# A build-time planner that counts all DMA queues as one pipe, lets row pairs interrupt dense products, and runs an FFN unit of the last chunk later

## The chip, the cores and the metric

The kernel runs on one core of a Trainium2 chip. The metric is the device time of one execution in microseconds (us), as the median of several runs. A profiled execution gives the trace: its span runs from the first to the last instruction, and its own time is a little longer than the span.

## The reference

A transformer layer for 2048 tokens of width 640: attention in a sliding window of 256 tokens with 32 heads of 20, then a feed-forward network (FFN) of width 1536 with a gated GELU, both behind a layer norm and with a residual. Everything is float32.

```python
def _A_ref(x, wqkv, wo):                       # H = 32; Dh = 20; W = 256
    qkv = (x @ wqkv).reshape(B, S, 3, H, Dh).transpose(2, 0, 3, 1, 4)
    q, k, v = qkv[0], qkv[1], qkv[2]
    scores = einsum("bhqd,bhkd->bhqk", q, k) * (Dh ** -0.5)
    mask = (idx[:, None] - idx[None, :] >= 0) & (idx[:, None] - idx[None, :] < W)
    p = softmax(where(mask, scores, -1e9), axis=-1)
    o = einsum("bhqk,bhkd->bhqd", p, v)
    return o.transpose(0, 2, 1, 3).reshape(B, S, D) @ wo
def _B_ref(x, w_gate, w_up, w_down):
    return (gelu(x @ w_gate) * (x @ w_up)) @ w_down

h  = x + _A_ref(layernorm(x), A_wqkv, A_wo)
h2 = h + _B_ref(layernorm(h), B_w_gate, B_w_up, B_w_down)
```

## The kernel before

**Dense products.** Every float32 operand of a large product is split into two float16 parts, high and low, and the product is three float16 matmuls (high by high, high by low, low by high) summed in PSUM (the helper `products`). These are the dense products: `qk` for the queries and keys of a chunk of 256 tokens, `vproj` and `wo_block` for a block of 128 tokens, and the FFN's. There are 16 blocks and 8 chunks. In rows of the trace the float16 weights are `w0`, `w1`, `w2`, `w3` (q, k, v, o) with `h` or `l` behind, and `xh`, `xl`, `oh`, `ol` are the parts of the normed input and of the attention's output.

**Attention.** A block has 8 units of 4 heads. For each unit the scores are computed twice: once to find each row's maximum (`maxima`, rows `ps<-kT,qT`), and once, with that maximum subtracted by two extra rows of qT, transposed for the exponential (`scores`, rows `ps<-qT,kT`). Two units use the two halves of TensorE's 128 rows at the same time; two such units are a row pair, mostly one of maxima for a later block and one of scores, 24 matmuls in all. Each of the two writes its own set of three PSUM banks, and a pair starts only when both sets are free. Behind maxima VectorE (DVE) masks and reduces (`mxs`) and so frees the set; behind scores ScalarE (ACT) takes the exponential into `pt` and frees the set, GpSimd (POOL) masks `pt`, and the values follow: 48 matmuls `ps<-pt,v` for two units, on columns of TensorE in groups of 32 (`value_lane`).

When the 8 units of a block have their maxima, `max_rows` splits them into `m16`, TensorE transposes them (`ps<-ident,m`), ACT copies the result to `mT`, and two DMAs on ACT's queue write it into the extra rows of qT. Only then can the block's first scores run.

**Turning.** `turned` transposes a block of x, of the attention's output (o) or of the normed h for use as a matmul operand: ACT casts to the high part `sph`, POOL subtracts to get the low part `spl`, and two transposing DMAs on SP's queue write both. There is one `sph` and one `spl`, so a cast waits until the transposing DMA of the cast before has read.

**FFN.** It works on 4 chunks of 512 tokens (c) and 3 groups of 512 inner columns (fg), 12 units (c, fg), each with `gate_up` and `down`. Except for two of them, gate and up use seven block products instead of eight on sums of weights and of tokens (`gate_up_sums`). The sums of a chunk's tokens are `token_sums`, written to `tTh`, `tTl` or to a part of the room of `kT`, which is free then. The list `SEQ` sets the order of the units; `feed_forward` issues the gate/up of one unit and then the down of the unit before. The weights of group 0 are split a second time late in the list, when `("up", 3, 2)` is done, since their room was used for group 2. The first FFN units also serve as filling for TensorE at the end of the attention.

**What sets the order of the work.** Nothing is ordered by hand. The program is written by lanes, Python generators whose steps each issue a few instructions, and while it is built a planner, the class `Clock`, keeps a planned time for each engine: `Engine.cost` gives each instruction's duration, `issue` advances the engine's time beyond the operands' planned times, and a DMA is planned to land some time after its issue. A lane's step is taken when its operands are ready in this plan. The order in which lanes are asked at each step is `order = early + outs + trans + sides + turn`; `turn` holds the three lanes that feed TensorE: `rows` (row pairs), `values` and `dense`. Once the v weights are split it was:

```python
elif pos["open"]:
    turn = [dense, values, rows]
elif nc.mode == "row":
    turn = [values, dense, rows]
elif nc.mode == "col":
    turn = [dense, rows, values]
else:
    turn = [rows, values, dense]
if W["v"].ready and not pos["open"] and pos["since"] and row_need() < nc.t["tensor"] + SOON:
    turn = [rows, values]
```

`pos["open"]` is 1 while a dense product is unfinished, `pos["since"]` counts products since the last row pair, and `row_need()` is the planned time at which the next pair could start. With `SOON = 2.0`, dense work is held back at a product's end when a pair is due within 2 us. The result is a fixed order of instructions on each engine; nothing is scheduled on the chip. All instructions are recorded through one helper, so their line in the trace is L211 (L226 in the changed file).

Of the kernel before, what the change touches and what calls it, by code (L numbers as in the profile page):

```python
# [55 lines left out]
class Clock:  # L56
# [6 lines left out]
    def __init__(self, nc):  # L63
        self.nc = nc
        self.t = dict.fromkeys(self.NOW, 0.0)
        self.wr, self.rd, self.rings = {}, {}, {}
        self.warm, self.win, self.use = False, 0, 0.0
        self.mode, self.half = "full", 0
        self.moved = dict.fromkeys(self.NOW, 0.0)
        self.port = {"vector": deque(maxlen=6), "gpsimd": deque(maxlen=6)}  # L70
        for e in self.NOW:
            setattr(self, e, Engine(self, e))
# [98 lines left out]
    def shares(reads, writes):  # L171
        big = [a for a in reads if a.free_size() > 1 and a.space != PSUM]
        return len(big) > 1 or (len(big) == 1 and not any(a.space == PSUM for a in reads)
                                and writes[0].free_size() > 8 and writes[0].space != PSUM)

    def issue(self, eng, cost, reads, writes, move=False):
        start = self.t[eng]
        boxes = [self.box(a) for a in reads], [self.box(a) for a in writes]
        for a, (k, b) in zip(reads, boxes[0]):
            start = max(start, self.latest(self.wr, k, b, eng))  # L180
            if a.space == PSUM:
                start = max(start, self.others(a, eng))
        for k, b in boxes[1]:
            start = max(start, self.latest(self.wr, k, b, eng), self.latest(self.rd, k, b, eng))
        if not move and (eng == "gpsimd" or eng == "vector" and self.shares(reads, writes)):
            for a, z in self.port["vector" if eng == "gpsimd" else "gpsimd"]:
                if a <= start < z:
                    start = z
            self.port[eng].append((start, start + cost))
        if move:  # L190
            self.t[eng] = start + move
            self.moved[eng] = max(self.moved[eng], start + 0.2) + cost
            end = self.moved[eng] + 1.7
        else:
            end = self.t[eng] = start + cost
        for k, b in boxes[0]:
            self.note(self.rd, k, b, eng, end)
        for k, b in boxes[1]:
            self.note(self.wr, k, b, eng, end)


class Engine:
# [23 lines left out]
    def cost(self, op, out, ins):  # L226
        n = out.free_size()
        if op.startswith("dma_start"):
            size = n * out.partition_size() * mybir.dt.size(out.dtype)
            return size / (300e3 if mybir.dt.size(out.dtype) == 4 else 150e3)  # L230
        half = mybir.dt.size(out.dtype) == 2 and ins and mybir.dt.size(ins[0].dtype) == 2
        if self.name == "tensor":
            n = ins[1].free_size()
# [31 lines left out]
def block_kernel(ctx: ExitStack, tc: tile.TileContext, x, wqkv, wo, wg, wu, wd, out):  # L265
    nc = Clock(tc.nc)
# [75 lines left out]
    FFBACK = dict(split_lane=0.4, scale_lane=0.4, chunk_lane=0.3)  # L342
    EARLY = 0.6
    PACE = 1.0
    SOON = 2.0

    def need(*reads, slots=(), when=None, eng="tensor"):

# [217 lines left out]
    W = {}  # L566
# [80 lines left out]
    def products(n, term, ready=None, at_=None):  # L647


        ps = [at_[0]] if at_ else []  # L650
        col = at_[1] if at_ else 0

        def start(i):
            if ready and not ready(i):
                return INF
            t = nc.ready([x for ab in term(i) for x in ab], "tensor")
            return t if ps else max(t, room("mm"))

        for i in range(n):
            yield ("tensor",), lambda i=i: start(i)  # L660
            if not ps:
                ps.append(bank("mm"))
            pos["open"] = 1
            m = term(i)
            for k, (l, r) in enumerate(m):
                if k:
                    yield pe()
                o = ps[0][:, col:col + r.free_size()]
                nc.tensor.matmul(o, l, r, start=(i == 0 and k == 0),
                                 stop=(i == n - 1 and k == len(m) - 1))  # L670
                pos["dense"] += r.free_size()
        pos["open"] = 0
        pos["since"] += 1
        return o

    ffk = const.tile([P, FG, 5], F32, name="ffk")
# [330 lines left out]
    def row_lane():  # L1007
        while True:
            yield ("tensor",), row_need
            gens = []  # L1010
            pos["since"] = 0
            for s, (f, x) in enumerate(row):
                (maxq if f is maxima else scoreq).remove(x)
                gens.append(f(*x, row_set(s)))
# [157 lines left out]
    def wo_out(j, nh, ps):  # L1172
# [6 lines left out]
        if b.halves < 2:  # L1179
# [6 lines left out]
    NCH = S // (CB * P)  # L1186
    hts, ga, tT = {}, {}, {}
    flags = set()
    SEQ = [(0, 0), (1, 0), (0, 1), (1, 1), (1, 2), (0, 2), (2, 2), (3, 2), (3, 1), (2, 1), (2, 0),
           (3, 0)]  # L1190
    POOL = (0, 1, 1, 0)

# [69 lines left out]
    def gate_up_sums(c, fg):  # L1262
# [9 lines left out]
        for w in ws:  # L1272
            tiles = {}
            for n, terms in enumerate(STEPS):
# [9 lines left out]
                for h in range(2):  # L1284
                    for m, x in enumerate(names):
                        yield ("tensor",), lambda: start(*x)
                        new = ps is None
                        if new:
                            ps = bank("mm")
                        pos["open"] = 1  # L1290
                        l, r, k = x
                        for p, (lw, rt) in enumerate(parts(w.part(l, k), tokens(c, r, k))):
                            if p:
# [5 lines left out]
                            pos["dense"] += 256  # L1299
                tasks.append(combine(n, w is ws[1], c, fg, ps, tiles, gels))  # L1300
                yield
        pos["open"] = 0

    def combine(n, up, c, fg, ps, tiles, gels):

# [408 lines left out]
    while dense.alive or sides or side or outs or tasks:  # L1714
# [11 lines left out]
        if not W["v"].ready:  # L1726
            att_first = maxq or nc.t["vector"] < nc.t["tensor"]
            turn = [rows, values, dense] if att_first else [dense, rows, values]
        elif pos["open"]:
            turn = [dense, values, rows]  # L1730
        elif nc.mode == "row":
            turn = [values, dense, rows]
        elif nc.mode == "col":
            turn = [dense, rows, values]
        else:
            turn = [rows, values, dense]
        if W["v"].ready and not pos["open"] and pos["since"] and row_need() < nc.t["tensor"] + SOON:
            turn = [rows, values]
        order = early + outs + trans + sides + turn
        for lane in order:  # L1740
            if lane.alive and lane.start(now):
# [59 lines left out]
```

## Time and profile before

| | before |
|---|---|
| median of 3 runs | 1013.43 us (1011.65 to 1015.23) |
| the profiled execution | 1011.27 us, span 1009.6 us |
| mean granted clock of TensorE | 0.988 |
| PE (matmuls) busy | 953.7 us, 94% |
| DVE, ACT, POOL busy | 730.7, 484.1, 238.1 us |
| DMA | 106.89 MB; SP's queue (q1) 35.8%, ACT's queue (q10) 4.4% of 16 engines |

Attention, with the projections between, runs to some 615 us of the span; the rest is FFN. Idle time is given with what ended it. A busy PE is not always a fast one: the granted clock says whether it ran at full or at half speed.

### The profile page before, as it was taken

How to read it: one execution, taken by the hardware profiler on the slowest of the kernel's cores; microseconds unless marked ns; L12 is line 12 of the kernel's file. 1: busy time of each engine (PE TensorE's matmuls, PEld its weight loads, DVE VectorE, ACT ScalarE, POOL GpSimd, SP SyncE). 2: the span in 40 equal slices, each digit the busy share in tenths (PEclk: the TensorE clock that was granted, in tenths of full speed). 3: DMA queues.
4: the chain of work that ended last, by engine and by line, in shares of the span. 5: the costliest groups of instructions: out<-in, count | busy, mean ns of one | idle time of the engine just before them, and what ended most of it. 6: DMA issues, size and time to landing. Idle time of an engine off the chain costs nothing.

```text
span 1009.6 us, 27335 instructions
## 1 busy us (share of the span) xinstructions
PE 953.7 (94%) x11687; PEld 737.4 (73%) x11687; DVE 730.7 (72%) x1393; ACT 484.1 (48%) x711; POOL 238.1 (24%) x336
## 2 busy tenths in 40 slices
PE   3997998899899999999998999999999999999998
PEld 2885666677687777777555656888788778888886
DVE  6986698686675666665998745979977969663563
ACT  6634656555556555655677663654322224231120
POOL 5201233544543433333434320000111200000000
PEclk9998998999999999999999999999999999999999
DMA  9446685543662533527467014252334323000002
GB/s 338 121 121 187 162 219 125 114 111 69 121 145 55 129 86 78 105 59 202 122 158 170 16 27 157 69 181 87 98 80 132 92 66 83 31 15 1 1 1 105
DMA packets 109305, 106.89 MB, mean 106 GB/s; under 512 B 59136, under 2 KB 79872, under 8 KB 107264
## 3 DMA queue, kind: packets, MB, share of 16 engines
q1 hardware_dynamic: 86080, 94.40, 35.8%
q10 hardware_dynamic: 23104, 10.75, 4.4%
q8 instruction: 91, 1.49, 0.6%
q14 instruction: 30, 0.25, 0.1%
HBM read 71.11 MB, written 20.97 MB: 91 GB/s over the span
## 4 chain that ended last, share of the span: by engine, by line
PE 54%; DVE 22%; DMA 10%; ACT 6%; issue 5%; POOL 2%; SPq 1%; ACTq 1%; DVEq 0%; POOLq 0%
PE ps L211 54%; DVE gel L211 4%; DVE mxs L211 3%; DVE kT L211 3%; DVE ps L211 2%; DMA lxn<-h_dram 2%; ACT pt L211 2%; DVE ht L211 2%; DMA qT<-mT 1%; DMA h0l<-spl 1%; ACT wsl L211 1%; DVE wu L211 1%; DMA wsl<-in_wd_dram 1%; DMA wsl<-in_wg_dram 1%; DVE gu L211 1%
## 5 line engine op out<-in xcount | busy, mean ns | idle before, releaser
L211 ACT ACTIVATE pt<-ps,esc 128x1536 f32<-128x1536 f32 (+2 forms) x128 | 186.4, 1460 | 77.3 <-PE ps L211 64.2
L211 POOL TENSOR_SCALAR_AFFINE_SELECT pt<-pt 128x512 f32<-128x512 f32 x240 | 149.2, 644 | 288.5 <-ACT pt L211 283.5
L211 DVE TENSOR_REDUCE mxs<-ps 128x4 f32<-128x1024 f32 (+1 forms) x128 | 150.5, 1179 | 2.0
L211 PEld LDWEIGHTS <-kT 62*128 62x128 f16 (+1 forms) x1920 | 126.6, 96 | 33.9 <-issue 11.6
L211 DVE COPY_PREDICATED ps<-mask,ps 128x512 f32<-128x512 int32 x112 | 77.4, 692 | 81.7 <-PE ps L211 80.8
L211 DVE TENSOR_TENSOR gel<-gel,ps 128x512 f32<-128x512 f32 x140 | 93.3, 684 | 46.9 <-PE ps L211 43.4
L211 PE MATMUL ps<-qT,kT 62*128 62x128 f16 x1440 | 102.6, 219 | 14.4 <-DMA qT<-mT 8.0
L211 PEld LDWEIGHTS <-gu 128*128 128x128 f16 x888 | 87.2, 99 | 38.2 <-issue 4.0
L211 PEld LDWEIGHTS <-wu 128*128 128x128 f16 x1080 | 105.6, 98 | 12.5 <-DVE wu L211 0.3
L211 PE MATMUL ps<-kT,qT 60*128 60x128 f16 x1440 | 106.2, 219 | 8.7 <-DVE mxs L211 6.5
L211 PEld LDWEIGHTS <-qT 60*128 60x128 f16 x1440 | 82.0, 95 | 41.6 <-issue 41.2
L211 PE MATMUL ps<-pt,v 128*21 128x128 f32 x2880 | 92.3, 276 | 2.4 <-ACT mT L211 1.5
L211 PEld LDWEIGHTS ps<-pt,v 128*21 128x21 f32 x2880 | 74.2, 101 | 16.8 <-issue 7.4
L211 DVE SCALAR_TENSOR_TENSOR ht<-ps,ffk,ht 128x320 f32<-128x320 f32 x96 | 51.8, 548 | 37.0 <-PE ps L211 35.3
L211 PE MATMUL ps<-xh,w0h 128*128 128x256 f16 x200 | 56.5, 282 | 5.9 <-ACT w0h L211 5.4
L211 PE MATMUL ps<-xh,w1h 128*128 128x256 f16 x200 | 56.4, 283 | 0.3 <-DVE qks L211 0.3
L211 PE MATMUL ps<-xl,w0h 128*128 128x256 f16 x200 | 56.4, 282 | 0.0
L211 PE MATMUL ps<-xl,w1h 128*128 128x256 f16 x200 | 56.1, 282 | 0.0
L211 PEld LDWEIGHTS <-ah 128*128 128x128 f16 x448 | 43.5, 98 | 16.8 <-issue 0.2
L211 PE MATMUL ps<-xh,w1l 128*128 128x256 f16 x200 | 55.7, 281 | 0.0
L211 PE MATMUL ps<-xh,w0l 128*128 128x256 f16 x200 | 55.6, 282 | 0.0
L211 ACT ACTIVATE gel<-gel,ffk 128x512 f32<-128x512 f32 x40 | 28.6, 719 | 45.8 <-DVE gel L211 45.7
(243 smaller groups left out, 2256.2 us busy)
## 6 DMA issues: line engine op xcount, KB each, us to landing
wsl<-in_wd_dram SPq DMA_DIRECT2D x28, 320.0 KB
wsl<-in_wg_dram SPq DMA_DIRECT2D x33, 256.0 KB
qk<-qks ACTq DMA_DIRECT2D x64, 128.0 KB
wsl<-in_wu_dram SPq DMA_DIRECT2D x30, 256.0 KB
qT<-qk SPq DMA_DIRECT2D x16, 320.0 KB
kT<-qk SPq DMA_DIRECT2D x16, 320.0 KB
ht<-in_x_dram SPq DMA_DIRECT2D x16, 320.0 KB
h_dram<-ht SPq DMA_DIRECT2D x16, 320.0 KB
```

Source lines behind the costliest of these rows:

```text
L211: r = real(*args, **kw)
```

## The change

Three things change in the planner and one list in the kernel.

- Every DMA, of whichever queue, takes its transfer time from one shared list of used stretches (`pipe`), starts 0.4 us after its issue, and lands 1.3 us after its transfer, or 3.3 us for a small one. The rates become 330 and 300 KB/us, and 90 for a transposing DMA, in place of 300 and 150 for each queue by itself.
- `turn` is always `[rows, values, dense]` once v is split. `pos["open"]`, `pos["since"]` and `SOON` are gone: a row pair or values may start between any two matmuls of a dense product, and dense work is never held back.
- In `SEQ` the unit (2, 1) moves from the tenth to the seventh place; (2, 2), (3, 2) and (3, 1) come one place later.

```diff
--- before.py
+++ after.py
@@ -66,7 +66,7 @@
         self.wr, self.rd, self.rings = {}, {}, {}
         self.warm, self.win, self.use = False, 0, 0.0
         self.mode, self.half = "full", 0
-        self.moved = dict.fromkeys(self.NOW, 0.0)
+        self.moved, self.used = dict.fromkeys(self.NOW, 0.0), []
         self.port = {"vector": deque(maxlen=6), "gpsimd": deque(maxlen=6)}
         for e in self.NOW:
             setattr(self, e, Engine(self, e))
@@ -173,6 +173,21 @@
         return len(big) > 1 or (len(big) == 1 and not any(a.space == PSUM for a in reads)
                                 and writes[0].free_size() > 8 and writes[0].space != PSUM)
 
+    def pipe(self, at, cost):
+
+        gaps = []
+        for a, z in self.used:
+            if at < a:
+                gaps.append((at, min(a, at + cost)))
+                cost -= gaps[-1][1] - at
+                if cost <= 0:
+                    break
+            at = max(at, z)
+        if cost > 0:
+            gaps.append((at, at + cost))
+        self.used = sorted(self.used[-150:] + gaps)
+        return gaps[-1][1]
+
     def issue(self, eng, cost, reads, writes, move=False):
         start = self.t[eng]
         boxes = [self.box(a) for a in reads], [self.box(a) for a in writes]
@@ -189,8 +204,8 @@
             self.port[eng].append((start, start + cost))
         if move:
             self.t[eng] = start + move
-            self.moved[eng] = max(self.moved[eng], start + 0.2) + cost
-            end = self.moved[eng] + 1.7
+            self.moved[eng] = self.pipe(max(self.moved[eng], start + 0.4), cost)
+            end = self.moved[eng] + (1.3 if cost > 0.05 else 3.3)
         else:
             end = self.t[eng] = start + cost
         for k, b in boxes[0]:
@@ -227,7 +242,9 @@
         n = out.free_size()
         if op.startswith("dma_start"):
             size = n * out.partition_size() * mybir.dt.size(out.dtype)
-            return size / (300e3 if mybir.dt.size(out.dtype) == 4 else 150e3)
+            if op.endswith("transpose"):
+                return size / 90e3
+            return size / (330e3 if mybir.dt.size(out.dtype) == 4 else 300e3)
         half = mybir.dt.size(out.dtype) == 2 and ins and mybir.dt.size(ins[0].dtype) == 2
         if self.name == "tensor":
             n = ins[1].free_size()
@@ -342,7 +359,6 @@
     FFBACK = dict(split_lane=0.4, scale_lane=0.4, chunk_lane=0.3)
     EARLY = 0.6
     PACE = 1.0
-    SOON = 2.0
 
     def need(*reads, slots=(), when=None, eng="tensor"):
 
@@ -660,7 +676,6 @@
             yield ("tensor",), lambda i=i: start(i)
             if not ps:
                 ps.append(bank("mm"))
-            pos["open"] = 1
             m = term(i)
             for k, (l, r) in enumerate(m):
                 if k:
@@ -669,8 +684,6 @@
                 nc.tensor.matmul(o, l, r, start=(i == 0 and k == 0),
                                  stop=(i == n - 1 and k == len(m) - 1))
                 pos["dense"] += r.free_size()
-        pos["open"] = 0
-        pos["since"] += 1
         return o
 
     ffk = const.tile([P, FG, 5], F32, name="ffk")
@@ -1008,7 +1021,6 @@
         while True:
             yield ("tensor",), row_need
             gens = []
-            pos["since"] = 0
             for s, (f, x) in enumerate(row):
                 (maxq if f is maxima else scoreq).remove(x)
                 gens.append(f(*x, row_set(s)))
@@ -1186,7 +1198,7 @@
     NCH = S // (CB * P)
     hts, ga, tT = {}, {}, {}
     flags = set()
-    SEQ = [(0, 0), (1, 0), (0, 1), (1, 1), (1, 2), (0, 2), (2, 2), (3, 2), (3, 1), (2, 1), (2, 0),
+    SEQ = [(0, 0), (1, 0), (0, 1), (1, 1), (1, 2), (0, 2), (2, 1), (2, 2), (3, 2), (3, 1), (2, 0),
            (3, 0)]
     POOL = (0, 1, 1, 0)
 
@@ -1287,7 +1299,6 @@
                         new = ps is None
                         if new:
                             ps = bank("mm")
-                        pos["open"] = 1
                         l, r, k = x
                         for p, (lw, rt) in enumerate(parts(w.part(l, k), tokens(c, r, k))):
                             if p:
@@ -1299,7 +1310,6 @@
                             pos["dense"] += 256
                 tasks.append(combine(n, w is ws[1], c, fg, ps, tiles, gels))
                 yield
-        pos["open"] = 0
 
     def combine(n, up, c, fg, ps, tiles, gels):
 
@@ -1726,16 +1736,8 @@
         if not W["v"].ready:
             att_first = maxq or nc.t["vector"] < nc.t["tensor"]
             turn = [rows, values, dense] if att_first else [dense, rows, values]
-        elif pos["open"]:
-            turn = [dense, values, rows]
-        elif nc.mode == "row":
-            turn = [values, dense, rows]
-        elif nc.mode == "col":
-            turn = [dense, rows, values]
         else:
             turn = [rows, values, dense]
-        if W["v"].ready and not pos["open"] and pos["since"] and row_need() < nc.t["tensor"] + SOON:
-            turn = [rows, values]
         order = early + outs + trans + sides + turn
         for lane in order:
             if lane.alive and lane.start(now):
```

The instructions are the same, but ACT loads its tables of functions 4 times instead of 8; their order changes on every engine. Three places follow, before and after apart.

First, PE at block 2. The row with `ident16` transposes the block's maxima; the rows of `w1h` and `w1l` are the dense product of keys in which it stands, and `LDWEIGHTS qT` with what follows begins the pair that has the block's first scores. Before:

```order
L211 MATMUL ps8_73<-ident16_77,m16_2073 64x128
L211 LDWEIGHTS w1h_281
L211 MATMUL ps8_73<-xl_674,w1h_281 128x256
L211 LDWEIGHTS w1l_282
L211 MATMUL ps8_73<-xh_673,w1l_282 128x256
L211 LDWEIGHTS w1h_281
L211 MATMUL ps8_73<-xh_673,w1h_281 128x256
L211 LDWEIGHTS w1h_281
L211 MATMUL ps8_73<-xl_674,w1h_281 128x256
L211 LDWEIGHTS w1l_282
L211 MATMUL ps8_73<-xh_673,w1l_282 128x256
L211 LDWEIGHTS qT_1005
```

After, the same transpose stands three rows ahead of these, in the output product of an earlier block (`w3`, `oh`, `ol`); the pair that begins with `LDWEIGHTS qT_958` belongs to maxima of block 3 and scores of block 1:

```order
L226 LDWEIGHTS oh_1762
L226 MATMUL ps8_73<-w3l_1306,oh_1762 128x320
L226 LDWEIGHTS ol_1763
L226 MATMUL ps8_73<-w3h_1305,ol_1763 128x320
L226 LDWEIGHTS oh_1762
L226 MATMUL ps8_73<-w3h_1305,oh_1762 128x320
L226 LDWEIGHTS oh_1762
L226 MATMUL ps8_73<-w3l_1306,oh_1762 128x320
L226 LDWEIGHTS qT_958
L226 MATMUL ps8_73<-kT_107,qT_958 128x128
L226 LDWEIGHTS kT_107
L226 MATMUL ps8_73<-qT_430,kT_107 128x128
```

Before, five dense matmuls stood between the transpose and the scores that need it, and pairs stood only at ends of products; after, a pair stands in the middle of a product, another pair and more dense work follow, and the first scores of block 2 come 37 dense matmuls, two pairs and a set of values after the transpose.

Second, ACT at the casts of `turned` in the middle of the attention: `sph` is the cast, `o32` and `xt` are its sources, `pt` an exponential, `qks` the copy of a query or key product. Before, `xt_2717` is block 12 of x:

```order
L211 CAST sph_3924<-o32_3627 128x640
L211 ACTIVATE pt_3935<-ps8_73,esc_109 128x1536
L211 ACTIVATE qks_4006<-ps8_73 128x512
L211 DMA qk50_3878<-qks_4006 128x2x256
L211 CAST sph_4011<-xt_2717 128x640
L211 DMA qk50_3878<-qks_4006 128x2x256
L211 COPY oT_4040<-ps8_73 128x256
L211 ACTIVATE pt_4014<-ps8_73,esc_109 128x1536
```

After, `xt_2446` is block 12 of x and `xt_2728` block 13:

```order
L226 CAST sph_3966<-xt_2446 128x640
L226 ACTIVATE v1_102<-ps8_73 128x16x20
L226 CAST sph_4008<-o32_3693 128x640
L226 ACTIVATE pt_3979<-ps8_73,esc_109 128x1536
L226 ACTIVATE qks_4054<-ps8_73 128x512
L226 DMA qk51_3965<-qks_4054 128x2x256
L226 ACTIVATE pt_4063<-ps8_73,esc_109 128x1536
L226 DMA qk51_3965<-qks_4054 128x2x256
L226 CAST sph_4135<-xt_2728 128x640
L226 COPY oT_4172<-ps8_73 128x256
```

The cast of o and the next cast of x now have two exponentials between them instead of one, and another cast of x stands close ahead of the cast of o.

Third, ACT in the FFN, at the token sums of the last chunk (`kT<-kT`, 4 casts) and the first copy of a gate/up unit (`COPY gel`). Before, the copy that follows is that of unit (3, 2), which uses these sums:

```order
L211 CAST sph_11990<-lxn_11839 128x640
L211 CAST kT_107<-gel_11778 128x2x256
L211 CAST kT_107<-gel_11742 128x2x256
L211 CAST kT_107<-kT_107 128x512 x4
L211 COPY gel_12161<-ps8_73 128x512
L211 ACTIVATE gel_12161<-gel_12161,ffk_85 128x512
```

After, the copy that follows at once is that of unit (2, 2), and that of (3, 2) is `COPY gel_12524`:

```order
L226 CAST kT_107<-kT_107 128x512 x4
L226 COPY gel_12163<-ps8_73 128x512
L226 ACTIVATE gel_12163<-gel_12163,ffk_85 128x512
L226 ACTIVATE gel_12232<-gel_12232,ffk_85 128x512
L226 ACTIVATE gel_12212<-gel_12212,ffk_85 128x512
L226 ACTIVATE gel_12178<-gel_12178,ffk_85 128x512
L226 COPY gel_12288<-ps8_73 128x512
L226 CAST ah_12133<-gel_12163 128x2x256
L226 CAST ah_12133<-gel_12232 128x2x256
L226 CAST ah_12133<-gel_12212 128x2x256
L226 CAST ah_12133<-gel_12178 128x2x256
L226 COPY gel_12524<-ps8_73 128x512
```

The token sums stay where they were, and a whole gate/up unit with its down stands between them and the unit that needs them.

## The prediction

> **What bounds the kernel now.** I read the page first: engine shares, slices, chain.
>
> ```profile
> span 1009.6 us, 27335 instructions
> PE 953.7 (94%) x11687; PEld 737.4 (73%) x11687; DVE 730.7 (72%) x1393; ACT 484.1 (48%) x711; POOL 238.1 (24%) x336
> PE 54%; DVE 22%; DMA 10%; ACT 6%; issue 5%; POOL 2%; SPq 1%; ACTq 1%; DVEq 0%; POOLq 0%
> ```
>
> TensorE bounds it. The change keeps every matmul, so it can only pay in the 56 us in which PE was idle, in the time at the lower clock, and in what switching between kinds of matmul costs. So next come the stretches, with PE busy after the length and the granted clock behind the engines:
>
> ```profile
> 0.00:25.00 25.00, 8.97 (x35) 5.25 (x36) 14.98 (x46) 16.43 (x36) 13.36 (x21) 1.00 0.92 341
> 75.00:100.00 25.00, 18.89 (x198) 14.62 (x196) 16.13 (x28) 10.66 (x19) 3.13 (x5) 0.86 0.65 184
> 150.00:175.00 25.00, 20.97 (x318) 15.29 (x318) 20.52 (x35) 13.90 (x17) 7.83 (x12) 0.86 0.65 133
> 275.00:500.00 225.00, 221.21 (x3782) 167.05 (x3782) 149.98 (x232) 128.97 (x153) 89.12 (x132) 1.00 0.45 109
> 800.00:825.00 25.00, 22.49 (x179) 18.05 (x178) 17.47 (x30) 6.12 (x10) 0.00 (x0) 0.93 0.30 106
> 825.00:1006.00 181.00, 181.00 (x1520) 148.38 (x1517) 112.43 (x188) 41.49 (x64) 0.00 (x0) 1.00 0.10 31
> ```
>
> Start-up loses 16 us and the change doesn't touch it. The last 181 us lose nothing, and 275 to 500 only 3.8. The loss sits in a few places where the clock dips. The same view on the five stretches at half clock (length, PE busy, clock):
>
> ```profile
> 80.30:87.10 6.80, 5.99 (x36) 0.50 0.72 215
> 152.00:158.80 6.80, 5.42 (x54) 0.50 0.90 224
> 264.60:268.00 3.40, 3.40 (x23) 0.50 0.52 133
> 527.40:530.80 3.40, 3.40 (x69) 0.50 0.12 36
> 814.10:817.50 3.40, 3.40 (x19) 0.51 0.50 194
> ```
>
> PE was busy for 21.6 us there at half speed, which is 10.8 us lost. Each stretch follows a wait. From PE's waits and the timeline (the bracket is the idle time ahead and what ended it):
>
> ```profile
> PE ps L211 <- DMA qT<-mT: 8.0, 3, 4.2
> PE ps L211 <- DVE mxs L211: 6.5, 9, 1.1
> PE ps L211 <- ACT pt L211: 6.3, 7, 2.5
> PE ps L211 <- DVE o L211: 1.0, 2, 0.7
> 72.81 0.24 PE L211 MATMUL ps<-ident,m 128*64 128x128 f16 x1
> 81.11 0.26 PE L211 MATMUL ps<-qT,kT 62*128 62x128 f16 x1 [4.19 <-DMA qT<-mT]
> 149.21 0.24 PE L211 MATMUL ps<-ident,m 128*64 128x128 f16 x1
> 153.38 0.29 PE L211 MATMUL ps<-qT,kT 62*128 62x128 f16 x1 [3.11 <-DMA qT<-mT]
> 261.41 0.72 ACT L211 CAST sph<-xt 128x640 f16<-128x640 f32 x1 [2.73 <-DMA oh<-sph]
> 263.90 0.21 PE L211 MATMUL ps<-qT,kT 62*128 62x128 f16 x1 [2.49 <-ACT pt L211]
> 527.02 2.45 PE L211 MATMUL ps<-pt,v 128*21 128x128 f32 x48 [1.08 <-ACT mT L211]
> 811.52 0.62 ACT L211 CAST kT<-kT 128x512 f16<-128x512 f32 x1 [4.89 <-DVE kT L211]
> 812.19 0.27 PE L211 MATMUL ps<-kT,gu 128*128 128x256 f16 x1 [1.98 <-ACT kT L211]
> 812.91 0.49 PE L211 MATMUL ps<-kT,gu 128*128 128x256 f16 x3 [0.46 <-DVE kT L211]
> ```
>
> The path from the transpose of a block's maxima to its first score took 8.30 us for block 0 and 4.17 for block 2. At 261 ACT stood behind a cast that needed a transposing DMA, so a score's exp came late. At 810 the FFN unit (3,2) reached its second step before its token sums were stored.
>
> The timeline also gives PE's prices:
>
> ```profile
> 293.76 0.27 PE L211 MATMUL ps<-xl,w1h 128*128 128x256 f16 x1
> 293.87 0.27 PE L211 MATMUL ps<-xh,w1l 128*128 128x256 f16 x1
> 294.07 0.23 PE L211 MATMUL ps<-kT,qT 60*128 60x128 f16 x1
> 294.12 0.21 PE L211 MATMUL ps<-qT,kT 62*128 62x128 f16 x1
> 294.44 0.21 PE L211 MATMUL ps<-kT,qT 60*128 60x128 f16 x1
> ...
> 308.02 0.30 PE L211 MATMUL ps<-w2l,xh 128*128 128x320 f16 x1
> 308.16 0.30 PE L211 MATMUL ps<-w2h,xl 128*128 128x320 f16 x1
> 308.39 0.23 PE L211 MATMUL ps<-kT,qT 60*128 60x128 f16 x1
> ...
> 309.02 0.22 PE L211 MATMUL ps<-qT,kT 62*128 62x128 f16 x1
> 309.17 0.31 PE L211 MATMUL ps<-w2h,xh 128*128 128x320 f16 x1
> ```
>
> Starts stand 0.11 us apart for 256 columns and 0.136 for 320; a row pair of 24 matmuls took 308.39 to 309.02. From the last dense matmul to a pair it is 0.23, so 0.095 above the step: that is a switch of kind. At 294.12 the pair stood for 0.3 us: only 1.83 us of work lay behind the pair before, and one of its PSUM sets was not free.
>
> **The change, part by part.** Distances below are matmuls counted in the order of the instructions, times these steps.
>
> *Switches.* The order has 324 changes of kind on PE before and 340 after: pairs begin inside an open product 81 times (never before), but stand next to the values more seldom. 16 x 0.095 = +1.5 us. [...]
>
> *Waits for mT.* Between the maxima's transpose and the first score of block 0 stand 3.7 us of work before and 7.9 after; for block 2 it is 0.6 and 7.8, block 1 has 4.2 and 5.7, and no later block has under 3.9. Block 0 lost 4.19 us idle and half of the 5.99 at half clock, 7.2 together; if the path is again 8.30, some 0.4 stays and the clock holds: -6.8. Block 2 lost 3.11 + 2.7 = 5.8, and its path of 4.17 is now covered: -5.8. The cover is dense products; if they run dry, these 12.6 us come back.
>
> *ACT behind the cast.* 2.49 idle + 1.7 at half clock = 4.2. After, two exps instead of one stand between that cast and the next, but two casts of another place now follow each other with only a v copy between. Ends 0 and -4.2; neither row is nearer, so I take the middle: -2.1.
>
> *The wait at 527.* 1.08 behind ACT and 1.7 at half clock: 2.8. ACT's copy of mT was late behind other work there and I can't read from the order that it won't be: ends 0 and -2.8, middle -1.4.
>
> *FFN units.* With (2,1) moved to the front, the last chunk's unit (3,2) comes one unit later, and its token sums are stored one gate/up unit (216 x 0.109 = 23.5 us) ahead instead of in its first step. The waits of 1.98 and 0.46 and 1.7 at half clock go: -4.1. Price: the second split of the group-0 gate and up weights still waits for (3,2), and has 13.1 + 23.5 + 13.1 = 49.7 us until (2,0) instead of 86. In the order its last piece stands 195 dense steps, 23.8 us, ahead of (2,0): nothing. If ACT and DVE fell behind by more, (2,0) would wait for the rest. Its loads on SP wait only for free slices, and stand ahead of that.
>
> *End of attention.* The last block's two transposes now have dense work between and behind them. PE stood there twice for `DVE o`, 1.0 us in all; what now stands between is 5 and 6 matmuls, some 0.8 us: -0.8.
>
> ACT's four table loads less lie there too; ACT is 48% busy and no wait of PE named here ends in one: nothing.
>
> *SP and POOL.* Both issue what they issued, in another order, SP with the weight loads spread between the transposing DMAs. Of DMAs, PE's list of waits names only `qT<-mT`, which ACT issues, so I price the moves on SP through ACT's cast alone; late transfers of x would show as a wait of the projections, and belong to case 2.
>
> *Short distances.* Before, 18 pairs stand 1.8 to 1.9 us behind the last one and lose 0.3 each: 5.4. After, 6 stand at 0.7 to 1.75 and 7 at 1.8 to 2.0; measured against 1.83 + 0.3, or 2.15, that would have been enough, they lose 5.2 + 1.6 = 6.8: +1.4.
>
> *Waits for maxima and exps, 87 to 150 us.* PE's waits of this stretch alone:
>
> ```profile
> PE ps L211 <- DVE mxs L211: 3.0, 5, 0.8
> PE ps L211 <- ACT pt L211: 1.7, 2, 1.4
> ```
>
> These are 4.7 us. Scores start some 12 us of work later, when less of the layernorms and weight scaling is left on DVE. Ends 0 and -4.7, and the middle for want of a nearer row: -2.4.
>
> *No slack.* A pair now starts at the matmul at which the plan has its sets free, not at the end of a product. The nearest rows are the pairs of 275 to 500, of which many were already placed at the plan's instant: 3.8 us over 57 pairs, 0.066 each. For the 81 that is +5.3. Ends: 0, and 0.3 each (the wait at 294.12) = +24.
>
> Sum: 1.5 - 6.8 - 5.8 - 2.1 - 1.4 - 4.1 - 0.8 + 1.4 - 2.4 + 5.3 = -15.2. The profiled execution took 1011.3 (span 1009.6 and 1.7 around it): 996.1. The median of the runs is 2.2 above it, 1013.4: **998**.
>
> **The clock rule.** The trace lets the clock fall after idle gaps of 1.5 to 4.2 us (the rows above). [...] The measured rule cuts both ways: a new wait of 2 us may cost nearly twice its length.
>
> **Rivals.**
> 1. *Slower: row pairs without slack wait.* If DVE and ACT run later than planned, every pair waits on its PSUM set, where a half-done product used to give up to 2 us of margin. Place: before each `kT,qT` row from 85 to 560 us. The other terms sum to -20.5, so over 127 pairs it decides from 0.16 us each; at 0.25 it is 31.8, and the time 1013.4 - 20.5 + 31.8 = 1025. For it: the 0.3 at 294.12. Against: 0.066 as a mean in the steady part.
> 2. *New waits of the same kind.* The order is new everywhere; one new wait the size of block 2's (5.8) and one the size of that at 261 (4.2) give 998 + 10 = 1008.
> 3. *The plan's DMA times still miss.* The changed order then leaves the mT waits and ACT's cast as they are (6.8 + 5.8 + 2.1 back): 1013, no change.
> 4. *All of it.* No slack costs nothing, the three halved terms come whole and half of the short distances goes: 998 - (5.3 + 2.1 + 1.4 + 2.4 + 3.4) = 983.
>
> **How the numbers follow.** Forecast (992 to 1005) 0.50; case 4 0.15; case 2 0.15; case 3 0.09; case 1 0.11. 0.3% is 3 us, about what runs of 1011.65 to 1015.23 can tell from no change, so faster means below 1010.4: 0.50 + 0.15 + 0.15 = 0.80; same 0.09; slower 0.11. The range takes in case 4 and most of 2 and 3: 983 to 1011, leaving out the slower case and the tails.
>
> **What would show it.** Clock 1.00 around the first scores and at 810; no wait of over 1 us for `qT<-mT`; no wait for `ACT kT` at (3,2); PE's idle below 42 us. I am wrong if the waits for `DVE mxs` and `ACT pt` together rise from 12.8 to over 25 (case 1), or if half-clock stretches stand at new places (case 2).

## The result, and the profile after

The changed kernel takes 1018.28 us (median of 7 runs, 1016.98 to 1024.46) where the kernel before takes 1013.13 (7 runs, 1010.13 to 1015.23): a ratio of 1.0067, 95% interval 1.0043 to 1.0092. It is slower by 0.67%; forecast were 998 us and a range of 983 to 1011. The profiled execution took 1018.28 us, 7.0 more than that of before.

The page of the changed kernel: span, engines, chain.

```profile
span 1016.2 us, 27314 instructions
...
PE 955.4 (94%) x11687; PEld 735.5 (72%) x11687; DVE 735.5 (72%) x1393; ACT 475.4 (47%) x707; POOL 239.2 (24%) x336
...
PE 70%; DMA 11%; DVE 8%; ACT 6%; issue 3%; ACTq 1%; POOL 1%; SPq 0%; DVEq 0%
```

The chain holds more of PE and as much of DMA as before (70% against 54%, 11 against 10), and DVE's part fell from 22% to 8%. PE's busy time grew by 1.7 us and the span by 6.6, so some 5 us are more idle time. The stretches (length, then busy time of PE, PEld, DVE, ACT and POOL, granted clock, DMA share, GB/s):

```profile
75.00:100.00 25.00, 21.41 (x202) 16.42 (x200) 13.05 (x25) 7.87 (x19) 0.27 (x1) 1.00 0.70 195
...
150.00:175.00 25.00, 19.08 (x258) 13.55 (x253) 15.55 (x39) 12.05 (x21) 6.13 (x8) 1.00 0.80 188
225.00:250.00 25.00, 20.18 (x340) 16.20 (x341) 14.47 (x25) 10.21 (x13) 9.49 (x13) 0.86 0.75 157
...
275.00:500.00 225.00, 214.94 (x3879) 163.61 (x3880) 152.49 (x219) 126.03 (x145) 92.35 (x137) 0.98 0.44 100
800.00:825.00 25.00, 25.00 (x208) 20.10 (x207) 20.97 (x36) 5.37 (x9) 0.00 (x0) 1.00 0.33 113
```

75 to 100 is better than before (21.41 against 18.89, clock 1.00 against 0.86), 800 to 825 loses nothing now, and 275 to 500, which lost 3.8 us of PE's time, loses 10.1. Half-clock stretches stand at five new places and not at one of the old:

```profile
115.60:119.00 3.40, 3.28 (x34) 2.11 (x34) 3.40 (x5) 1.37 (x3) 0.56 (x1) 0.50 0.74 200
122.40:125.80 3.40, 3.40 (x27) 2.52 (x24) 2.40 (x7) 0.95 (x2) 1.19 (x2) 0.50 0.49 172
241.90:248.70 6.80, 5.68 (x58) 4.22 (x59) 3.00 (x4) 3.75 (x5) 3.56 (x5) 0.50 0.82 149
310.10:313.60 3.50, 3.50 (x44) 2.26 (x44) 0.29 (x1) 0.18 (x1) 0.81 (x1) 0.51 0.57 95
371.60:378.40 6.80, 3.77 (x63) 2.78 (x65) 1.38 (x2) 1.49 (x2) 1.23 (x2) 0.50 0.54 62
```

PE's waits (total, times, longest), without the start:

```profile
PE ps L226 <- ACT pt L226: 10.6, 6, 4.8
...
PE ps L226 <- ACT oT L226: 4.7, 11, 1.0
...
PE ps L226 <- DVE qks L226: 4.4, 6, 1.7
PE ps L226 <- DMA oh<-sph: 4.1, 2, 3.6
PE ps L226 <- DVE mxs L226: 3.4, 8, 1.0
PE ps L226 <- DMA ol<-spl: 1.8, 2, 1.6
```

No `qT<-mT` is left among them. New are products that wait for the transposed output of the attention, and two long waits for an exp. The timelines of ACT, PE and SP at these four places (a bracket is the idle time ahead and what ended it; SPq rows are issues of DMAs):

```profile
161.86 1.42 SPq L226 DMA_DIRECT2D kT<-qk  x3
...
164.89 1.32 SPq L226 DMA_TRANSPOSE h0h<-sph  x1
...
173.13 0.73 ACT L226 CAST sph<-xt 128x640 f16<-128x640 f32 x1 [5.89 <-DMA h0h<-sph]
...
175.35 0.21 PE L226 MATMUL ps<-qT,kT 62*128 62x128 f16 x1 [3.25 <-ACT pt L226]
...
228.19 3.48 SPq L226 DMA_DIRECT2D kT<-qk  x3
...
233.60 2.50 SPq L226 DMA_TRANSPOSE h0h<-sph  x1
...
240.80 0.73 ACT L226 CAST sph<-o 128x640 f16<-128x640 f32 x1 [6.55 <-DMA h0h<-sph]
...
243.02 0.26 PE L226 MATMUL ps<-qT,kT 62*128 62x128 f16 x1 [4.82 <-ACT pt L226]
...
301.27 1.81 SPq L226 DMA_TRANSPOSE ol<-spl  x1
...
309.42 0.31 PE L226 MATMUL ps<-w3h,ol 128*128 128x320 f16 x1 [1.60 <-DMA ol<-spl]
...
374.63 0.45 PE L226 MATMUL ps<-w3h,oh 128*128 128x320 f16 x1 [3.59 <-DMA oh<-sph]
```

At 164.89 SP issues a transposing DMA behind seven loads of qT and kT. It has read `sph` at 173.1, 8 us later; until then ACT stands before its next cast with an exp behind it, and PE waits 3.25 us for that exp. The same happens at 238, behind seven loads from 226.6 on. At 308 and 371 PE waits for the transposed block itself; at 371 the DMA was issued late, since SP had stood for a store whose room the next load on its queue takes (SP's waits from 361 to 372 us):

```profile
SPq L226 <- DMA h_dram<-ht: 7.5, 1, 7.5
```

The four waits sum to 13.3 us, and the stretches at 241.9, 310.1 and 371.6 behind three of them cost half of PE's 12.95 us there, 6.5 more. Behind the wait at 172 the clock held (1.00 from 170.2 to 177.0).

What the loads of qT and kT take can be read from the packet records: nearly all packets of 8192 bytes are theirs (1920 of 1956). In the changed kernel such a group is 200 packets from 161.3 to 171.8 us, 1638 KB in 10.5 us = 156 KB/us, and 240 packets from 293.6 to 306.1, 157 KB/us. In the kernel before the groups nearest to these two were of 120 packets, from 144.4 to 151.2 (146) and from 215.9 to 222.3 (152); a group of 240 there, at 458, ran at 158. The price for them was 150 KB/us in the plan before and is 300 now. The price also sets the pace, since from the third chunk on a load is issued only when the plan's transfers of SP end within 1 us:

```python
if c > 1:
    yield ("sync",), lambda: nc.moved["sync"] - PACE
```

So loads are sent out about twice as fast as the chip moved them here (planned at 300 KB/us, moved at 156 and 157), and what SP issued next landed behind the rest: the loads ahead of the transposing DMA of 164.89 ended at 171.8, and it had packets under way until 172.2.

### The profile page after: what moved, and what is told of

Read it like the earlier page. It is cut to its first block, busy times and chain, and to the rows that moved or that the text cites. A ratio compares the mean times of both kernels' runs of the same rounds, so it can differ in the third digit from the quotient of the medians.

```text
span 1016.2 us, 27314 instructions
## 1 busy us (share of the span) xinstructions
PE 955.4 (94%) x11687; PEld 735.5 (72%) x11687; DVE 735.5 (72%) x1393; ACT 475.4 (47%) x707; POOL 239.2 (24%) x336
## 4 chain that ended last, share of the span: by engine, by line
PE 70%; DMA 11%; DVE 8%; ACT 6%; issue 3%; ACTq 1%; POOL 1%; SPq 0%; DVEq 0%
PE ps L226 70%; ACT pt L226 3%; DVE mxs L226 2%; DMA xt<-in_x_dram 2%; DMA h0h<-sph 2%; DMA wsl<-in_wd_dram 1%; DMA qk<-qks 1%; DMA ol<-spl 1%; ACTq L226 1%; ACT wsl L226 1%; DVE ps L226 1%; DMA wsl<-in_wu_dram 1%; DMA lxn<-h_dram 1%; DMA wsl<-in_wg_dram 1%; DMA qT<-mT 1%
## 5 line engine op out<-in xcount | busy, mean ns | idle before, releaser
L226 PE MATMUL ps<-qT,kT 62*128 62x128 f16 x1440 | 102.0, 220 | 11.0 <-ACT pt L226 10.6
L226 PE MATMUL ps<-pt,v 128*21 128x128 f32 x2880 | 94.4, 277 | 4.0 <-POOL pt L226 1.5
L226 DVE SCALAR_TENSOR_TENSOR qks<-ps,qks 128x512 f16<-128x512 f32 (+1 forms) x48 | 28.7, 599 | 36.1 <-ACT qks L226 35.9
```

Of the source, the lines that this page charges most:

```text
L226: r = real(*args, **kw)
```

## Experiments

Theory A: transfers that the plan prices too low land late, and ACT and PE wait for them. Theory B: the row pairs that start without slack cost the time. Theory C came later: the planner is greedy, so that any change draws a new order.

Two numbers help to read them. The *plan's end* is the planned end of the last matmul, which the program computes while it is built; it is no time of the chip. The *distance* is how much later than planned the last instruction of DVE ended in the trace: 22.3 us in the kernel before, 31.1 in the changed one. By its own clock the changed plan ends 2.1 us earlier than the old one (981.7 against 983.8), and the chip is 8.8 us further behind it. Each distance is that of the one profiled execution. Along the changed kernel's run it grows from 14 to 21 us at 238, from 21 to 24 at 308 and from 24 to 27 at 371.

### The three parts alone

`p_pipe` is the kernel before with `pipe`, the new rates and landing times; `p_turn` has only the new `turn`; `p_seq` only the new `SEQ`. The fourth kernel, `a_f16`, is the changed one with a rate put back:

```diff
-            return size / (330e3 if mybir.dt.size(out.dtype) == 4 else 300e3)
+            return size / (330e3 if mybir.dt.size(out.dtype) == 4 else 150e3)
```

> The kernel before with the transfers part alone (one pipe for all queues, the new prices, the new landing times); turn and unit order as before. Theory A (late transfers): the plan now prices 16-bit loads at 300 KB/us, while the groups of 8192-byte packets in both traces run at about 150; so the loads of qT and kT go out 5 or 6 in a row, the transposing DMAs behind them in the same queue land 5 to 6.4 us after their issue, and ACT's cast into sph and the products with oh and ol wait for them. Those four waits of the changed kernel are 13.3 us (3.25, 4.82, 1.60, 3.59) and their half-clock stretches some 6 more, against 12.6 us of waits for qT<-mT that go. A expects this part alone to show both: waits of that kind over 1.5 us present, no wait over 1 us for qT<-mT, 1014 to 1021 us. Theory B (row pairs without slack cost the time): this part alone has only the gains, 1000 to 1005 us, and no wait over 1.5 us for sph or oh.

Measured: 1048.55 us, ratio 1.0357 (1.0309 to 1.0405). It is far above both expectations. The plan itself ends 29.2 us later than before and the distance is 31.1. PE's longest waits for transfers are now for the loads themselves:

```profile
PE ps L226 <- DMA kT<-qk: 8.9, 3, 4.3
...
PE ps L226 <- DMA oh<-sph: 4.7, 2, 3.2
```

> The kernel before with the turn part alone (row pairs may start inside a dense product); prices and unit order as before. Theory A: 16 more switches of kind make +1.5 us, and the short waits for qks, oT and pt some more; the waits for qT<-mT and the stall at 810 us stay: 1013 to 1018 us, no transposing DMA later than 4.5 us. Theory B: this part carries the loss, which in the changed kernel outweighs 12.6 us of mT waits and 4 us at 810: 1025 us or more.

Measured: 1020.45 us, ratio 1.0106 (1.0053 to 1.0159), between the two. The distance is 23.5, as before, but the plan ends 7.2 us later. B's reason is not in the trace: waits for `mxs` and `pt` rose only from 12.8 to 16.2 us.

> The kernel before with the order of the last chunk's units alone. Attention is planned as before, so only the stall at 810 us (4.1 us lost in the prediction's count) can go: both theories expect 1008 to 1010 us, and no idle time over 1 us on PE between 700 and 900 us. 1013 would say that the stall at 810 us is not the unit's cost or comes back elsewhere.

Measured: 1009.02 us, ratio 0.998 (0.9949 to 1.0012). The stall of the unit is gone:

```profile
700.00:900.00 200.00, 200.00 (x1716) 167.54 (x1714) 162.21 (x312) 63.86 (x98) 17.01 (x16) 1.00 0.29 78
```

The median moved by 0.8 us, with an interval that reaches from 5.1 less to 1.2 more, so the 4.1 us are neither shown nor refuted in the time. Up to the FFN PE's order is that of the kernel before, and yet the half-clock stretch of 3.4 us at 527 is one of 6.8 us at 541 in this execution: on one order, single executions differ by that much.

> The changed kernel with one number put back: 16-bit loads priced at 150 KB/us (as before, and as measured for qT and kT) and not at 300; pipe, landing times, turn and unit order as changed. Theory A: the plan spreads the loads or works on until the transposes have landed; no wait over 1.5 us behind a cast into sph or for oh and ol between 100 and 400 us; 1000 to 1008 us. Theory B: the row pairs still start without slack, so 1015 to 1020 us. A third way: one pipe at 150 KB/us is dearer than the chip, since those loads keep only about 9 of 16 engines busy at a time, so that the plan holds PE's rows back and the loss moves to later starts: 1015 to 1030 us with the waits for sph gone.

Measured: 1037.23 us, ratio 1.0252 (1.0207 to 1.0297), the third way. The distance fell from 31.1 to 3.7 us, and PE waits no more than 1.5 us for an exp and for no DMA into `oh` or `ol`: most of what this plan was missed by came from the price. But the truer plan ends 46.5 us later. The rate put back is that of every 16-bit transfer but the transposing ones, so of the stores of `qk` too. The "9 of 16 engines" above is a mean over packet times; the view of the stretch 161.3 to 171.8 in the changed kernel gives a DMA share of 0.97, in which the long packets count (some of 256 bytes were under way for 5.6 us there).

So the parts don't add: +38.7, +10.6 and -0.8 us alone, +5.2 together.

### The loads cut, the order kept

To see what the late transfers cost without a new plan, `a_cut` keeps every engine's instructions in the order of the changed kernel, and only moves less:

```diff
+                nc.half_load = which == 1 and c > 2
                 nc.sync.dma_start(to[64 * par + DH * m:64 * par + DH * (m + n)],
                                   dv[par, 0:DH * n])
...
+            n = o.partition_size() // 10
+            return real(o[:n], i[:n])
```

> The changed kernel with every engine's instructions in the same order; only the real loads of kT from the fourth pair of blocks on move a tenth of their partitions (2 of 20, 4 of 40), so that its scores are computed from old keys. With qT in full that is 1081 KB a group where 1966 KB were moved, about what the plan's price of 300 KB/us allows for. The third group (161 to 172 us) stays whole, as a control. Theory A (loads at twice the planned price, transposing DMAs land late behind them): the wait at 172 us stays (3.2 us), those at 238 (4.82) and 307 (1.60) go and the one at 371 (3.59, where SP also waited for a tile of the residual) shrinks or stays; with their half-clock stretches (three of 3.4 us, 1.7 lost in each) 6 to 14 us less than the changed kernel: 1004 to 1012 us. Theory B (row pairs without slack): the same waits in the same places, 1016 to 1020 us.

Measured: 1004.87 us, ratio 0.9944 (0.9921 to 0.9967), 12.3 points per thousand below the changed kernel. ACT and PE of `a_cut` at the first two places:

```profile
171.70 0.72 ACT L228 CAST sph<-xt 128x640 f16<-128x640 f32 x1 [6.06 <-DMA h0h<-sph]
...
173.91 0.26 PE L228 MATMUL ps<-qT,kT 62*128 62x128 f16 x1 [3.41 <-ACT pt L228]
...
238.80 0.72 ACT L228 CAST sph<-o 128x640 f16<-128x640 f32 x1 [3.62 <-DMA h0h<-sph]
...
241.01 0.21 PE L228 MATMUL ps<-qT,kT 62*128 62x128 f16 x1 [1.88 <-ACT pt L228]
```

The control stays (3.41), the wait at 238 shrinks to 1.88, and no wait for `oh` or `ol` is left. At the fourth place SP's wait for the store, which stood behind the loads as well, is 2.5 us instead of 7.5:

```profile
SPq L228 <- DMA h_dram<-ht: 2.5, 1, 2.5
```

The view by stretches:

```profile
241.90:248.70 6.80, 6.21 (x119) 4.71 (x118) 5.65 (x9) 3.88 (x5) 2.80 (x5) 1.00 0.38 87
...
275.00:500.00 225.00, 219.39 (x3976) 165.51 (x3975) 159.88 (x233) 132.96 (x156) 95.99 (x143) 1.00 0.39 96
```

The clock holds here, and the distance ends at 17.3 instead of 31.1: 13.8 us, all of it won between 225 and 380 us. This is theory A shown with one thing changed. The row pairs stand where they stood, so theory B can't explain it. It isn't the whole distance to the forecast: `a_cut` is 0.56%, some 6 us, below the kernel before, where 15.2 were forecast. The wait at 172 is still in it, and so are longer waits for `oT` and `qks` (4.1 and 4.0 us, 2.7 and 0.3 in the kernel before), which remain although the loads are cut.

### The transposing DMA on another queue

```diff
+        if op == "dma_start_transpose" and "sph" in args[1].tensor.name:
+            real = self.clock.nc.scalar.dma_start_transpose
```

> The changed kernel with the same order of all work but one: the transposing DMA of the high half (sph) is issued by ACT right behind its cast, not by SP, so that it goes through ACT's queue and doesn't stand behind the loads of qT and kT in SP's. Theory A in its narrow form (it is the order within one queue): the waits at 172, 238 and 307 us go, for 39 issues of about 1.2 us on ACT, which is busy 47%: 1004 to 1016 us. If it is the sixteen DMA engines' own backlog, whatever the queue: the waits stay, and ACT's issues come on top: 1018 to 1030 us. Theory B: no gain either, 1018 to 1030 us, but the transposing DMAs land within 3 us.

Measured: 1055.36 us, ratio 1.0439 (1.0401 to 1.0478). It doesn't tell what it was made for, as it brought waits of its own. SP's list of waits from 321 to 335 us, and PE's row of the timeline behind it:

```profile
SPq L225 <- DMA xh<-sph: 12.1, 1, 12.1
```

```profile
336.74 0.45 PE L225 MATMUL ps<-w3h,ol 128*128 128x320 f16 x1 [7.06 <-DMA ol<-spl]
```

SP stood 12.1 us for a transposing DMA that ACT had issued, and what made it wait is not shown. One thing can be read: the high half that ACT issued at 320.87, with SP's loads of kT from 314.90 on still running, had its last packet at 325.7, 4.9 us later. On a queue of its own it was late as well. Up to 480 us, five of ACT's transposing DMAs ran beside 79 or more load packets of SP's queue; their last packets came 4.9 to 7.0 us after their issue, those of the others 2.1 to 4.0. So the backlog is not only one of the order within one queue.

### Is the order a matter of a nudge?

```diff
-SWITCH = 0.095
+SWITCH = 0.100
```

> The kernel before with one constant of the plan nudged: a switch of kind on PE priced at 0.100 us, not 0.095, which is no change of what the chip does. Theory C (the plan is greedy and any change of a price re-draws the whole order; the order of before is a good draw): another order with a time of its own, 1018 to 1026 us, worse by the plan's own clock (its end moves from 983.8 to 991.0) and with new waits at new places. If the order does not hang on such nudges: 1011 to 1015 us.

Measured: 1010.73 us, ratio 0.9993 (0.9967 to 1.0019). Half a miss: the order is another (320 changes of kind instead of 324, half-clock stretches at 80, 159 and 613 us), but the time is the same. The plan ends 7.2 us later and the distance is 7.5 less (14.8). A later end of the plan is therefore not by itself a slower kernel.

### A price for the queue's drain, and the five constants

`m1` lets a 16-bit transfer that doesn't transpose take the common pipe at 300 KB/us while its own queue drains at 150. `k37c` has other constants instead, and `m1_k37` has both.

```diff
-            self.moved[eng] = self.pipe(max(self.moved[eng], start + 0.4), cost)
+            at = max(self.moved[eng], start + 0.4)
+            self.moved[eng] = max(self.pipe(at, cost), at + cost * self.slow)
...
+            if mybir.dt.size(out.dtype) == 2:
+                k.slow = 2.0
```

```diff
-    LAT = 0.18
+    LAT = 0.175
-    NW, AHEADQ = 3, 6
+    NW, AHEADQ = 3, 7
-    AHEAD, APART = 0.2, 1.0
-    OUT, PREP, RAMPMAX, FFPREP, LATE = 0.75, 0.55, 0.25, 0.2, 0.4
+    AHEAD, APART = 0.3, 1.0
+    OUT, PREP, RAMPMAX, FFPREP, LATE = 0.8, 0.55, 0.25, 0.15, 0.4
```

> The changed kernel with a price that separates what theory A and the third way of the run before speak of: a 16-bit load takes the common pipe at 300 KB/us, but its own queue drains at 150; and five of the plan's constants set so that its own end comes early (981.8 us, by its own clock, where with the others' values most orders end at 1010 to 1035). Theory A with C: transposing DMAs are planned where they land, the plan's clock falls behind the chip's by less than 12 us (22.3 before, 31.1 in the changed kernel), and the time is 994 to 1006 us. Theory B: row pairs start without slack here as well, so the plan is missed by 25 us or more: 1012 to 1020 us.

Measured: 999.13 us (995.28 to 1000.38), ratio 0.9877 (0.9843 to 0.9911). It beats both kernels, and the distance of 12.0 is at the bound that was expected. In its trace (span 997.1 us) PE's only wait for a turned block is this row of its waits:

```profile
PE ps L227 <- DMA ol<-spl: 0.8, 2, 0.5
```

ACT's casts still wait for `h0h` (12.0 us, the longest 7.5), but PE's longest wait for an exp is 1.6 us.

> The changed kernel with the drain of the queue alone (a 16-bit load takes the pipe at 300 KB/us, its own queue drains at 150); the plan's five constants as in the changed kernel. The plan's own end is then 1000.3 us (981.7 in the changed kernel). Theory A: what the price repairs is the distance of the chip from the plan, 31.1 us in the changed kernel, so it falls to 10 to 16 us and the time, 5.5 us behind the last matmul, is 1016 to 1022 us: a truer plan, but a longer one. If the gain of the run before came from the price as such: 998 to 1006 us. Theory B: the distance stays at 25 us or more, 1030 us or more.

Measured: 1014.95 us, ratio 1.0031 (1.0003 to 1.0059). The time is 1 us and the distance (5.4) 4.6 us below what theory A gave; the two other expectations are further off.

> The changed kernel with the five constants of the run before alone; 16-bit loads at 300 KB/us in pipe and queue, as changed. The plan's own end is 1001.3 us. Theory A: the distance of the chip from the plan stays at 25 us or more and transposing DMAs make ACT's casts or the products with oh and ol wait: 1031 to 1040 us. If the gain of the run before came from the constants: 1000 to 1010 us, with a distance of under 16 us.

Measured: 1054.76 us, ratio 1.0434 (1.0396 to 1.0472), later than expected; the loads that come late are now waited for directly:

```profile
PE ps L226 <- DMA kT<-qk: 18.8, 5, 5.0
```

Plan's end + distance, and the time, of the four:

| | 16-bit loads at 300 KB/us in pipe and queue | queue drains at 150 |
|---|---|---|
| constants as changed | 981.7 + 31.1, 1018.28 | 1000.3 + 5.4, 1014.95 |
| the five constants | 1001.3 + 44.4, 1054.76 | 981.8 + 12.0, 999.13 |

The price takes 26 and 32 us off the distance in the two rows. The profiled executions of `m1` and `k37c` were the fastest of their runs, 4 us below the median each; at the medians it would be some 22 and 36. Whether the time follows depends on where the plan ends, which the constants decide, in no direction that these runs could foretell: they make it end 19.6 us later with the one price and 18.5 earlier with the other. So the best of the four owes its place to both, and its constants are a lucky draw, not an insight.

## Why the prediction was wrong

The time of PE beyond its work (each matmul by its step and 0.095 per switch), by stretches, from the two traces:

| us of the span | before | after |
|---|---|---|
| 0 to 75 | 22.9 | 24.0 |
| 75 to 175 | 24.8 | 25.1 |
| 175 to 275 | 13.2 | 13.1 |
| 275 to 400 | 6.9 | 16.7 |
| 400 to 675 | 19.8 | 19.3 |
| 675 to 975 | 6.0 | 0.4 |

The differences sum to +5.0, and the work grew by 1.6: the last matmul ends 6.6 us later.

- *Switches* (+1.5): the work measures 912.4 and 914.0, +1.6. Right.
- *FFN units* (-4.1): nothing is idle around 810, and 675 to 975 lost 5.6 us less. Right, with a little more than expected.
- *Waits for mT* (-12.6): they are gone, as forecast. But 75 to 175 lost as much as before. The wait of 3.25 that ends at 175 stands there now, the two half-clock stretches at 115.6 and 122.4 cost 3.3, and short waits fill the rest.
- *Waits at 87 to 150* (-2.4): the two waits that it prices, for `mxs` and `pt`, fell from 4.7 to 2.4, as forecast. But others that it left out came in their place, and all waits of the stretch rose from 5.4 to 8.9:

```profile
PE ps L226 <- DVE qks L226: 3.7, 4, 1.7
PE ps L226 <- DVE dg L226: 1.6, 1, 1.6
PE ps L226 <- DVE mxs L226: 1.4, 2, 1.0
PE ps L226 <- ACT pt L226: 1.0, 2, 0.8
```

- *The wait at 527* (-1.4) and *End of attention* (-0.8): waits for `mT` fell from 1.5 to 0.3 us and no half-clock stretch is left after 400 us, but 400 to 675 lost only 0.5 us less. PE's waits for `DVE o` went from 1.0 to 0.9. *Short distances* (+1.4) can't be told from the waits for `mxs`.
- *No slack* (+5.3) and case 1: `mxs` and `pt` together are 14.0 us (12.8 before), of which 8.1 are the two exps behind a late cast. Without those, 5.9. Case 1 did not happen; the row pairs' own waits fell, and those for `oT` and `qks` rose instead, from 3.0 to 9.1 us together. No term had these, and what makes them is not shown.
- *SP and POOL*, "I price the moves on SP through ACT's cast alone", together with *ACT behind the cast* (-2.1, ends 0 and -4.2): this is the step that failed. The old wait at 261 went as hoped, but the term had no end above nothing, although the change halves the planned time of the very loads that stand ahead of the transposing DMAs. The packets of 8192 bytes, which gave 150 KB/us in the trace of before, were never held against the new 300. The four waits that came of it are 13.3 us and some 6.5 at half clock; `a_cut`, which leaves the first of them, takes 13.8 back.
- *Case 2* was the mechanism, but mis-sized: two waits, +10, and a chance of 0.15. It was four from transfers alone. With wrong DMA times in the plan read as case 3, "no change", only case 1, with its 0.11, gave a slower kernel. Case 3 should have reached into a loss as well: wrong times that let the plan run ahead make new waits, and don't only keep the old.
- *The clock rule*: three of the four new waits cost clock as well as idle time, but that of 3.25 us cost none, although the rule had gaps of 1.5 to 4.2 us cost it (and its own row at 527 shows 1.08). That wait lay across two windows of the grid described at the end; in `a_cut` its counterpart of 3.41 us left one window emptier, and 6.8 us at half clock followed. So by these two runs the place on the grid counts as well as the length. The two windows of the changed kernel, and the one of `a_cut`:

```profile
170.20:173.60 3.40, 1.90 (x17) 1.41 (x16) 0.00 (x0) 0.47 (x1) 0.00 (x0) 1.00 0.93 174
173.60:177.00 3.40, 1.65 (x32) 1.45 (x32) 1.18 (x2) 3.40 (x5) 2.62 (x3) 1.00 0.76 183
```

```profile
169.10:172.50 3.40, 1.41 (x13) 0.97 (x11) 0.00 (x0) 0.80 (x2) 0.00 (x0) 1.00 0.82 177
```

- Of the signs named, the clock at the first scores and at 810 and the waits for `qT<-mT` came as forecast; PE's idle time is 60.8 us, not below 42, and half-clock stretches stand at new places.

Left open is why the parts alone cost so much more than all together. The plan's end accounts for it in numbers (29.2 of the 38.7 us of `p_pipe`, 7.2 of the 10.6 of `p_turn`), but why a plan without holding back dense work suits the new prices better was not tried.

## What to carry to other kernels

When a planner's price is changed, hold the new figure against the same transfers in the trace: bytes over time of a whole group, since a planned time that is too short also sends the loads out too fast. Here the harm fell on the transposing DMAs that SP issued next: their last packets came 6.2 to 7.5 us after the issue, at most other places 2.1 to 4.5. Split a planner's result into its own end and the chip's distance from it; the first is a draw that small changes re-draw, the second shows whether the prices are true. To test a suspected transfer, keep the order of instructions and change only the bytes.

## What was not expected of the hardware

- In the changed kernel the last packet of a transposing DMA came 2.1 to 4.5 us after SP began to issue it at most places up to 340 us, but 6.2 to 7.5 us behind the loads at 165, 234 and 300. Some packets of 256 bytes of the one issued at 164.9 were under way for 5.6 us (166.6 to 172.2), while others of the same DMA took 0.02.
- Short waits added up for the clock. Ahead of 115.6 no gap is over 1 us, yet the stretch is at half speed (0.50). In the window before it PE was busy for 1.72 of 3.40 us, and nearly the same ahead of 371.6:

```profile
112.20:115.60 3.40, 1.72 (x20) 1.17 (x19) 1.91 (x4) 3.24 (x6) 2.02 (x3) 1.00 0.86 200
368.20:371.60 3.40, 1.87 (x30) 1.13 (x28) 2.46 (x3) 2.30 (x3) 1.23 (x2) 1.00 0.32 78
```

In the kernel before, 2.19 was enough to keep the clock:

```profile
537.70:541.10 3.40, 2.19 (x35) 1.56 (x34) 3.33 (x12) 2.04 (x6) 1.10 (x3) 1.00 0.57 137
```

The bound is not sharp: a window of `m1_k37` kept it with 1.67, and the changed kernel's own window at 173.6 with 1.65. From 27 us on, all half-clock stretches in the trace of before begin on one grid of 3.41 us, and so do those of the changed kernel. Each of them follows a window of its grid with PE busy for some 1.9 us or less, and the emptiest windows that kept the clock had 2.19 in the kernel before and 1.65 in the changed one. No window had to be idle as a whole: half of it was enough, in pieces (1.68 us of 3.40 ahead of 115.6).
